# 52 spare matmuls of the identity with the mask in three places of TensorE's early queue, in a fused attention and feed-forward kernel

## The chip, the cores and the metric

The kernel runs on one core of one Trainium2 chip. The metric is the device time of one execution in microseconds, the median of three runs; lower is better. The engines are named as the profile names them: PE is TensorE, DVE is VectorE, ACT is ScalarE, POOL is GpSimd, SP is SyncE, which here only issues DMAs.

## The reference, cut to what matters

```python
# q, k, v: (B, H, S, D) = (4, 8, 576, 64); M_prev: (B, H, D, D); z_prev: (B, H, D)
scores = q @ k.T / sqrt(D), causal mask          # per batch and head
local  = softmax(scores) @ v
q_p    = where(q > 0, q, exp(q) - 1) + 1
mem    = (q_p @ M_prev) / (q_p . z_prev + 1e-6)
g      = sigmoid(beta)
x      = g * mem + (1 - g) * local               # (2304 tokens, 512)
h      = maximum(x @ w_in, 0)                    # w_in  (512, 2048)
out    = (h * h) @ w_out                         # w_out (2048, 512)
```

## The kernel before

**The tiling.** The 2304 tokens are cut into nine blocks of 256. Block 0 holds the first 64 tokens of each of the four batches; blocks 1 to 8 are two a batch. `first_tokens` computes the attention of block 0 (two groups `g`, each of two batches). `attention(b, p, tiles, ...)` computes the attention of the later tokens for batch `b` and head pair `p`. For batches 0 and 1 it runs twice a head pair, over the query tiles 1 and 2 (called lo below) and over the tiles 3 and 4 (hi). `moe(n)` is the feed-forward part of a block: "up" matmuls of 256 columns (L653 to L655, 192 a block) and "down" matmuls of 512 columns (L643 to L645, 96 a block). A product is made of three matmuls of high and low parts, so each weight is split once into two parts by ACT and DVE (`split_weight`, L163 to L169), and loaded in stages, as buffers come free.

**The order.** The program is recorded as a merge of `attention` for batch 0, lo, with the weight steps, then of `moe(0)` with more attention. A scheduler with a timeline of its own then sets the static order of each engine, and of the DMAs on SP's queue. Every engine works through its list in order, and what stands at its head waits for its operands. A change of the recorded program on one engine therefore changes the order on all of them.

**Buffers that the prediction speaks of.** Scores `sp` lie in a PSUM tile with the tag `s`, of which there is one, so the scores of the next group wait until DVE has read the last ones (L485). The tag `up` has two PSUM buffers, shared by the up products, the transposes `px` of the next block's tokens (L620, L622) and the transposes `px` and `pxa` of the first attention. Evacuation of `px` is done by ACT (`xh`, L625) and DVE (`xl`, L626). The tag `acc` has two PSUM buffers, those of the down products. The values `vv` of a head pair have one SBUF buffer, read by L399 and by L414 and L416.

**Operands of the new matmuls.** `identb` is the 128x128 identity in bf16, `mask` a 128x576 bf16 tile with 0 and -1e30; both exist before and are complete in the first 2.7 us.

Of the kernel before, what the change touches and what calls it, by code (L numbers as in the profile page):

```python
# [8 lines left out]
F32 = mybir.dt.float32  # L9
# [10 lines left out]
DM, FF = 512, 2048  # L20
NTOK = B * S
P = 128
# [50 lines left out]


FIRST = 4
AFTER = mybir.DependencyInfo(mybir.DependencyClass.NoSync, mybir.DependencyReason.DATA)
WHOLE = mybir.DependencyInfo(mybir.DependencyClass.Sync, mybir.DependencyReason.DATA)


def ORD(merge, attn, na, wsteps, first, order):  # L80
    merge((attn(0, 1), 12), (wsteps(13), 12))
    merge((attn(1, FIRST), 52), (wsteps(33), 20), (first(), 18))
    for _ in attn(FIRST, len(order)):
        pass
# [6 lines left out]
def fused_kernel(ctx: ExitStack, tc: tile.TileContext, t0_d, zt_d, kk_d, qv_d, beta, w_in, w_out, out):  # L91
    nc = tc.nc
# [5 lines left out]
    ps = ctx.enter_context(tc.tile_pool(name="ps", bufs=1, space=bass.MemoryType.PSUM))  # L98
# [6 lines left out]
    identb = cp.tile([P, P], BF16, name="identb")  # L105
    nc.vector.tensor_copy(identb, idt)
    mask = cp.tile([P, MW], BF16, name="mask")
# [87 lines left out]
    def weights():  # L195
        n0 = 0
        for n, ex in STG:
            n1 = n0 + n + len(ex)
            dpl = ctx.enter_context(tc.tile_pool(name=f"wd{n0}", bufs=1, reuse_waits="tile"))
            plain = range(n0 + len(ex), n1) if XF else range(n0, n0 + n)  # L200
            heads = []
            for m in range(n0, n1):
                if m in wt:
                    continue
                two = PAIR and m % 2 == 0 and m in plain and m + 1 in plain and m >= PAIR - 1
                wp[m] = dpl.tile([P, 2, 1024 if two else 512], F32R, name=f"w{m}")
                heads.append(m)
                for u in range(2 if two else 1):
                    wt[m + u] = wp[m][:, :, u * 512 : (u + 1) * 512]
            with ExitStack() as st:  # L210
                tp = st.enter_context(tc.tile_pool(name="tp", bufs=1, reuse_waits="tile")) if n0 == 0 else None
                spl = st.enter_context(tc.tile_pool(name=f"ws{n0}", bufs=1, reuse_waits="tile")) if n else None
                where = list(ex) + [spl] * n if XF else [spl] * n + list(ex)
                if n0 == 0:
                    first_tokens(tp, lambda: load_weight(heads[len(raw)], where[heads[len(raw)]]))
                    yield
                for m in range(n0, n1):
                    if m in heads:
                        if m not in raw:
                            load_weight(m, where[m - n0])  # L220
                        split_weight(m)
                    yield
            n0 = n1

    def first_tokens(tp, ahead):
        me, ze, se, xe, ye = ([nc.gpsimd if c == "p" else nc.vector for c in t] for t in TE)
        xh = mo.tile([P, NK, BLK], F32R, tag="xh", name="xh", bufs=2)
# [2 lines left out]
        ng = B // GB  # L230
        bc = [P, GN, D]
        tr, sp, wt0, wx = ({} for _ in range(4))
# [3 lines left out]
        for step in SEQ.split():  # L236
# [6 lines left out]
            else:  # L243
                g = int(step[1])
# [14 lines left out]
        def scores(g):  # L259
            sp[g] = sp0[:, g]  # L260
            qd = tr[g][:, : 2 * GD].rearrange("p (r i d) -> p i r d", r=2, i=GN)
            for i in range(GN):
                for h in range(2):
                    hd = slice(h * D, (h + 1) * D)
                    nc.tensor.matmul(sp[g][hd, i], qd[hd, i, 0], qd[hd, i, 1], start=True, stop=True)

        def phi(g):
            qn, zb = part(g, 2, 1), part(g, 3, 1)
            wt0[g] = tp.tile([P, GN, P], F32, tag="w", name="w", bufs=2)
            f = wt0[g][:, :, D:]  # L270
            t2 = tp.tile([P, GN], F32, tag="t2", name="t2", bufs=2)
            nc.scalar.activation(f, qn, AF.Exp)
            me[g].tensor_scalar(out=f, in0=f, scalar1=1.0, scalar2=None, op0=ALU.min)
            nc.vector.scalar_tensor_tensor(out=f, in0=qn, scalar=0.0, in1=f, op0=ALU.max, op1=ALU.add)
            ze[g].tensor_tensor(out=zb, in0=zb, in1=f, op=ALU.mult)
            nc.vector.reduce_sum(out=t2, in_=zb, axis=AX.X)
            nc.vector.tensor_scalar(out=t2, in0=t2, scalar1=1e-6, scalar2=None, op0=ALU.add)
            nc.vector.reciprocal(t2, t2)
            nc.vector.tensor_tensor(out=t2, in0=t2, in1=gpb, op=ALU.mult)
            se[g].tensor_tensor(out=f, in0=f, in1=t2[:, :, None].to_broadcast(bc), op=ALU.mult)  # L280
# [40 lines left out]

        sp0 = ps.tile([P, ng, GN, D], F32, tag="s", name="sp0")
        for g in range(ng):
            scores(g)
            phi(g)
        for g in range(ng):
            softmax(g)
# [18 lines left out]
    def attention(b, p, tiles, ld, after, early, sfull, full):  # L346
# [3 lines left out]
        tl = tiles[-1]  # L350
# [75 lines left out]
        for grp in (tiles[:2], tiles[2:]):  # L426
            ng = len(grp)
# [25 lines left out]
        row = {}  # L453

        def scores(group):
            sps = ps.tile([P, 2, 512], F32, tag="s", name="sp")
            c = 0
            at_col = []
            for i, ka, kb in group:
                qc = slice(QT[i][0] - D, sum(QT[i]) - D)  # L460
                cs = slice(c, c + kb - ka)
                at_col.append(cs)
                with tc.high_priority():
                    for x, (qt, kt) in enumerate(terms):
                        for h, hd in enumerate(heads):
                            mm = nc.tensor.matmul(  # L466
                                sps[:, h, cs], qt[hd, qc], kt[hd, ka:kb], start=x == 0, stop=x == len(terms) - 1
                            )
                            if behind:
                                tc.add_manual_dep(mm.ins, behind.pop().ins.name, AFTER, reason="a batch comes late")  # L470
                            while parts:
                                tc.add_manual_dep(mm.ins, parts.pop().ins.name, WHOLE, reason="a batch starts whole")
                c = cs.stop
            for (i, ka, kb), cs in zip(group, at_col):
                q0 = QT[i][0]
                if ka == 0:
                    row[i] = (
                        at.tile([P, 2, S], F32, tag="e", name="e", bufs=EB),
                        at.tile([P, 2, 2], F32, tag="mx", name="mx", bufs=4),
                        at.tile([P, 2], F32, tag="sm", name="sm", bufs=4),  # L480
                    )
                e, mx, _ = row[i]
                s = int(ka > 0)
                for h in range(2):
                    nc.vector.tensor_tensor_reduce(  # L485
                        out=e[:, h, ka:kb],
                        in0=sps[:, h, cs],
                        in1=mask[:, 448 - q0 + ka : 448 - q0 + kb],
                        scale=-0.125,
                        scalar=3e38 if s == 0 else mx[:, h, 0:1],  # L490
                        op0=ALU.add,
                        op1=ALU.min,
                        accum_out=mx[:, h, s : s + 1],
                    )

        for i in [t for t in TORD if t in tiles]:
            q0, n = QT[i]
            ke = q0 + n
            for group in SGROUP[i]:
                scores(group)  # L500
# [9 lines left out]
            if full:  # L510
# [3 lines left out]
                for b0 in range(0, 2 * nb, 4):  # L514
                    bn = min(4, 2 * nb - b0)
                    px = ps.tile([P, 4, P], F32, tag=PXT, name="pxa", bufs=2)
                    for x in range(bn):
                        h, c = divmod(b0 + x, nb)
# [38 lines left out]
            acc = ps.tile([P, 2, 2, D], F32, tag="av", name="acc", bufs=2)  # L557
            if full:
                s3 = acc[:, :, 0]
                for h in range(2):  # L560
                    hd = slice(h * D, (h + 1) * D)
# [143 lines left out]
                live[0][2] += 1  # L705

    blocks = [(None, 0)] + [(b, k) for b in range(B) for k in range(2)]
    xq, last, behind = [], [], []
    wg = weights()
    wn = [0]  # L710

# [21 lines left out]
    def attn(i0, i1):  # L733
        for i in range(i0, i1):
            ld = nxt.pop()

            def after():
                if i + 1 < len(order):
                    nxt.append(loads(*order[i + 1]))

            yield from attention(*order[i], ld, after, i < NEARLY, i < NES, i < NEF and max(order[i][2]) < 4)
# [67 lines left out]
```

## Time and profile before

| | us |
|---|---|
| median of three runs | 601.08 (600.86 to 603.04) |
| the profiled execution | 602.37 |
| its span, first to last instruction | 600.6 |
| PE busy in the span | 552.1 (92%) |
| DVE busy | 404.9 (67%) |
| ACT busy | 327.1 (54%) |

The profile is of one execution, whose own time lies 1.77 us above its span and 1.29 us above the median. Busy shares are averages over the whole span: DVE is full in the first part and nearly idle in the last quarter, PE the other way round, so the table alone doesn't say which engine sets the time. [...]

### The profile page before, as it was taken

Reading aid. Unit: us, or ns where it says so; the run is one execution under the profiler, and the core shown is the slowest. Engines: PE = TensorE matmul, PEld = TensorE weight load, DVE = VectorE, ACT = ScalarE, POOL = GpSimd, SP = SyncE. Lnnn points to the kernel's source line nnn. Section 1 sums busy time; section 2 is a strip of 40 time slices with the busy share of each in tenths; the row PEclk is TensorE's granted clock in tenths of the full one; section 3 lists DMA queues with packets and bytes.
Section 4 is the critical chain, followed back from the end, with each engine's and each line's share of the span. In section 5 each row is a group of like instructions: output and inputs, shape, how many; then the busy total and the mean of one; then the engine's idle time right before and its main releaser. Section 6 shows DMA issues by size and latency. Waiting matters only on the chain.

```text
span 600.6 us, 11532 instructions
## 1 busy us (share of the span) xinstructions
PE 552.1 (92%) x4198; PEld 482.5 (80%) x4198; DVE 404.9 (67%) x1285; ACT 327.1 (54%) x747; POOL 170.4 (28%) x139
## 2 busy tenths in 40 slices
PE   2478999799999999999999989999989999999997
PEld 2357887588888788788888888878879999998996
DVE  5999997888879798988789789897873001101000
ACT  3689885585767575855776646556351223213212
POOL 2502222044431424313332332223322321221221
PEclk9997999899999999999999999999999999999999
DMA  8947754666566575674565564564523100100000
GB/s 278 407 173 290 247 159 121 144 155 156 129 132 144 135 179 142 143 189 128 120 131 137 143 135 131 123 152 106 110 61 98 36 1 24 48 1 13 24 0 36
DMA packets 127576, 76.28 MB, mean 127 GB/s; under 512 B 99360, under 2 KB 112672, under 8 KB 127520
## 3 DMA queue, kind: packets, MB, share of 16 engines
q1 hardware_dynamic: 127520, 75.55, 47.6%
q8 instruction: 33, 0.54, 0.4%
q14 instruction: 23, 0.19, 0.1%
HBM read 42.63 MB, written 8.78 MB: 86 GB/s over the span
## 4 chain that ended last, share of the span: by engine, by line
PE 40%; DVE 31%; DMA 14%; ACT 8%; issue 4%; SPq 1%; POOL 1%; ACTq 0%; DVEq 0%
PE oacc L643 6%; PE oacc L645 6%; PE oacc L644 6%; PE up L653 6%; PE up L654 6%; PE up L655 6%; DVE a L545 5%; DVE e L485 4%; DMA vv<-in_qv_dram 4%; ACT e L505 3%; DMA aT<-a 3%; DMA qm<-in_qv_dram 3%; DVE w L169 3%; DVE memx L585 2%; PE sp L466 2%
## 5 line engine op out<-in xcount | busy, mean ns | idle before, releaser
L653 PE MATMUL up<-xh,w 128*128 128x256 f32 x576 | 167.2, 290 | 3.3 <-ACT aF L525 2.7
L654 PE MATMUL up<-xl,w 128*128 128x256 f32 x576 | 166.8, 290 | 0.0
L655 PE MATMUL up<-xh,w 128*128 128x256 f32 x576 | 165.8, 288 | 0.0
L668 POOL TENSOR_TENSOR gl<-r,gh 128x512 fp32r<-128x512 f32 x72 | 98.0, 1362 | 205.9 <-DVE gh L667 133.4
L505 ACT ACTIVATE e<-e,mx 128x320 f32<-128x320 f32 (+3 forms) x128 | 77.8, 609 | 86.3 <-DVE mx L485 45.0
L653 PEld LDWEIGHTS up<-xh,w 128*128 128x128 f32 x576 | 112.1, 195 | 8.3 <-ACT aF L525 3.1
L643 PE MATMUL oacc<-w,gh 128*128 128x512 f32 x288 | 115.5, 401 | 2.1 <-DVE gh L667 2.1
L654 PEld LDWEIGHTS up<-xl,w 128*128 128x128 f32 x576 | 112.2, 195 | 3.4 <-issue 0.9
L644 PE MATMUL oacc<-w,gh 128*128 128x512 f32 x288 | 113.8, 395 | 0.0
L655 PEld LDWEIGHTS up<-xh,w 128*128 128x128 f32 x576 | 112.2, 195 | 1.4 <-issue 0.4
L645 PE MATMUL oacc<-w,gl 128*128 128x512 f32 x288 | 110.5, 397 | 0.3 <-POOL gl L668 0.3
L661 POOL TENSOR_TENSOR r<-r 128x512 f32<-128x512 f32 x40 | 48.0, 1199 | 160.1 <-ACT r L659 156.4
L659 ACT ACTIVATE r<-up 128x512 f32<-128x512 f32 x72 | 42.2, 587 | 93.6 <-PE up L655 86.0
L667 DVE CAST gh<-r 128x512 fp32r<-128x512 f32 x40 | 16.9, 422 | 109.0 <-ACT r L663 108.0
L545 DVE SCALAR_TENSOR_TENSOR a<-e,a 128x128 f16<-128x128 f32 x120 | 71.8, 620 | 26.4 <-ACT a L543 26.1
L643 PEld LDWEIGHTS oacc<-w,gh 128*128 128x128 f32 x288 | 54.4, 189 | 12.3 <-DVE gh L667 2.4
L645 PEld LDWEIGHTS oacc<-w,gl 128*128 128x128 f32 x288 | 53.3, 188 | 13.3 <-issue 1.7
L644 PEld LDWEIGHTS oacc<-w,gh 128*128 128x128 f32 x288 | 54.4, 189 | 8.5
L543 ACT ACTIVATE a<-e 128x128 f16<-128x128 f32 x120 | 55.7, 519 | 4.3 <-DMA aT<-a 3.3
L485 DVE CUSTOM_DVE_ANT_0 e<-sp,mask 128x320 f32<-128x320 f32 (+3 forms) x128 | 47.5, 413 | 0.1
L575 PE MATMUL acc<-vs,aT 128*128 128x128 f16 x308 | 36.9, 220 | 0.0
L572 PE MATMUL acc<-vs,aT 128*128 128x64 f16 x308 | 35.5, 193 | 0.0
(127 smaller groups left out, 873.6 us busy)
## 6 DMA issues: line engine op xcount, KB each, us to landing
raw<-in_w_in_dram SPq DMA_DIRECT2D x11, 512.0 KB, 7.4
vv<-in_qv_dram SPq DMA_DIRECT2D x16, 320.0 KB, 3.3
raw<-in_w_out_dram SPq DMA_DIRECT2D x9, 512.0 KB, 7.0
kd<-in_kk_dram SPq DMA_DIRECT2D x16, 288.0 KB, 3.2
out_dram<-o SPq DMA_DIRECT2D x16, 256.0 KB, 2.0
xd<-memx SPq DMA_DIRECT2D x31, 128.0 KB, 1.9
xn<-xd SPq DMA_DIRECT2D x14, 256.0 KB, 2.8
qm<-in_qv_dram SPq DMA_DIRECT2D x8, 321.0 KB, 3.1
```

The costliest lines, as they stand in the source:

```text
L485: nc.vector.tensor_tensor_reduce(out=e[:, h, ka:kb], in0=sps[:, h, cs], in1=mask[:, 448 - q0 + ka : 448 - q0 + kb], scale=-0.125, scalar=3 ...
L505: ex = nc.scalar.activation(e[:n, h, :ke], e[:n, h, :ke], AF.Exp, bias=bs, scale=-1.0, accum_out=sm[:n, h : h + 1])
L543: nc.scalar.mul(av[:, :, o0 : o0 + w], x, SC)
L545: nc.vector.scalar_tensor_tensor(out=av[:, :, o0 + w : o0 + 2 * w], in0=x, scalar=SC, in1=av[:, :, o0 : o0 + w], op0=ALU.mult, op1=ALU.sub ...
L643: nc.tensor.matmul(acc[t], gh[:, u, ts], w_out_op(f, 0), start=f == 0, stop=False)
L644: nc.tensor.matmul(acc[t], gh[:, u, ts], w_out_op(f, 1), start=False, stop=False)
L645: nc.tensor.matmul(acc[t], gl[:, u, ts], w_out_op(f, 0), start=False, stop=f == NF - 1)
L653: nc.tensor.matmul(up[:, u, :], w_in_op(f, k, 0), xh[:, k, :], start=k == 0, stop=False)
L654: nc.tensor.matmul(up[:, u, :], w_in_op(f, k, 0), xl[:, k, :], start=False, stop=False)
L655: nc.tensor.matmul(up[:, u, :], w_in_op(f, k, 1), xh[:, k, :], start=False, stop=k == NK - 1)
L661: nc.gpsimd.tensor_tensor(out=r, in0=r, in1=r, op=ALU.mult)
L668: nc.gpsimd.tensor_tensor(out=gl, in0=r, in1=gh.bitcast(F32), op=ALU.subtract)
```

## The change

`spin(n, ins)` issues `n` matmuls of `identb` with the first 512 columns of `mask` into a PSUM tile `spun` with the tag `acc`, which nothing reads. Each has a dependency on an instruction that only orders the two in the schedule, and makes no engine wait. It is called three times: 14 after the scores of the second group of the first tokens, 28 after the scores of batch 0, pair 0, lo, and 10 ahead of the scores of batch 0, pair 2, lo, after DVE's read of the scores before them.

```diff
+SPIN = [14, 28, 10]
...
+    def spin(n, ins):
+        if not spun:
+            spun.append(ps.tile([P, DM], F32, tag="acc", name="spun", bufs=2))
+        for _ in range(n):
+            mm = nc.tensor.matmul(spun[0], identb, mask[:, :DM], start=True, stop=True)
+            tc.add_manual_dep(mm.ins, ins.ins.name, AFTER, reason="keeps the clock")
+
+    spun = []
+
     def first_tokens(tp, ahead):
...
         for g in range(ng):
-            scores(g)
+            mm = scores(g)
+            if g == ng - 1:
+                spin(SPIN[0], mm)
             phi(g)
...
         def scores(group):
+            if (b, p) == (0, 2) and tl == 2:
+                with tc.high_priority():
+                    spin(SPIN[2], reads[0])
             sps = ps.tile([P, 2, 512], F32, tag="s", name="sp")
...
+            if (b, p) == (0, 0) and tl == 2:
+                spin(SPIN[1], mm)
...
-                    nc.vector.tensor_tensor_reduce(
+                    read = nc.vector.tensor_tensor_reduce(
...
+                    if c == cs.stop and h == 0:
+                        reads[:] = [read]
```

Three places show how the static order changes. Lines of the change are numbered 10 to 20 higher than those of before: L466 is then L482, L485 is L503, L653 is L673.

The first place is PE's queue at the start. Before, the scores of the first tokens (L265) and of pair 0 (L466) are followed by the transposes of the first tokens' weights (L304):

```order
L265 MATMUL sp_155<-tr_118 64x64 x16
L265 MATMUL sp_155<-tr_119 64x64 x16
L466 MATMUL sp<-kd,qm 128x320 x2
L466 MATMUL sp<-kd,qm 128x192 x2
L304 MATMUL px_221<-identr,w 128x128 x4
```

With the change 14 pairs of a weight load and a matmul (L230) stand ahead of pair 0's scores, and 28 behind them; one pair of each stands here:

```order
L275 MATMUL sp_155<-tr_118 64x64 x16
L275 MATMUL sp_155<-tr_119 64x64 x16
L230 LDWEIGHTS identb
L230 MATMUL spun<-mask,identb 128x512
...
L482 MATMUL sp<-kd,qm 128x320 x2
L482 MATMUL sp<-kd,qm 128x192 x2
L230 LDWEIGHTS identb
L230 MATMUL spun<-mask,identb 128x512
...
L315 MATMUL px_236<-identr,w 128x128 x4
```

The third ten stand between the last transposes of pair 1 (L540) and the first up matmul of block 0; nothing else is new on PE.

The second place is PE's queue at the end of block 0, at batch 0, pair 1, hi. Before, its second scores (512 columns) follow its first ones (448 and 64 columns) with only `vt`, `pm` and two transposes between them:

```order
L466 MATMUL sp<-kd,qm 128x448 x2
L466 MATMUL sp<-kd,qm 128x64 x2
L403 LDWEIGHTS vx
L403 MATMUL vt<-identb,vx 128x128
L434 MATMUL pm<-qm,pe 128x130 x2
L622 MATMUL px<-identr,memx 128x128 x2
L466 MATMUL sp<-kd,qm 128x512 x2
L653 MATMUL up<-xh,w_1003 128x256
```

With the change the transposes of the next block have moved here too, and 38 up matmuls stand ahead of the second scores:

```order
L482 MATMUL sp<-kd,qm 128x448 x2
L482 MATMUL sp<-kd,qm 128x64 x2
L640 MATMUL px<-identr,xn 128x128 x3
L642 MATMUL px<-identr,memx 128x128
...
L416 LDWEIGHTS vx
L416 MATMUL vt<-identb,vx 128x128
L447 MATMUL pm<-qm,pe 128x130 x2
L673 MATMUL up<-xh,w_1056 128x256
...
L674 MATMUL up<-xl,w_98 128x256
L482 MATMUL sp<-kd,qm 128x512 x2
```

Both orders have 252 feed-forward matmuls ahead of the 448-column scores. Ahead of the next pair's first scores (pair 2, hi) there are 296 before and 322 with the change. Ahead of the memory product `pm` of batch 1, pair 1, lo, there are 549 and 535, and ahead of the last attention's `pm` 1648 and 1653.

The third place is DVE's queue at the same time. Before, the reduction of the values of pair 0, hi (L399) stands ahead of the reads of that pair's 512-column scores (L485):

```order
L545 SCALAR_TENSOR_TENSOR a<-e,a 128x2x64
L545 SCALAR_TENSOR_TENSOR a<-e,a 128x2x384
L399 TENSOR_REDUCE vx<-vv 128x1
L485 ISA e,mx<-sp,mask,mx 128x512
L485 ISA mx 128x1
L485 ISA e,mx<-sp,mask,mx 128x512
L485 ISA mx 128x1
L401 TENSOR_SCALAR vx<-vx 128x1
L389 SCALAR_TENSOR_TENSOR pe<-qm,pe 128x256
```

With the change those reads (L503), the last weight parts (L170) and the sums of `acc` (L597) stand ahead of it (L412):

```order
L503 ISA e,mx<-sp,mask,mx 128x512
L503 ISA mx 128x1
L503 ISA e,mx<-sp,mask,mx 128x512
L503 ISA mx 128x1
L170 TENSOR_TENSOR w_1207<-xw,w_1207 128x256
L402 SCALAR_TENSOR_TENSOR pe<-qm,pe 128x256
L170 TENSOR_TENSOR w_1207<-xw,w_1207 128x256
L597 TENSOR_REDUCE s_980<-acc 128x128
L597 TENSOR_REDUCE s_1012<-acc 128x128
L412 TENSOR_REDUCE vx<-vv 128x1
L565 SCALAR_TENSOR_TENSOR a<-e,a 128x2x64
L605 SCALAR_TENSOR_TENSOR memx<-s_980,sm,memx 128x64 x2
```

The last weight part is row 224 of DVE's list before and row 245 with the change; weights come later, attention of batch 0 earlier.

## Rows read from the trace of the kernel before

**Rows 1.** The page, 40 slices of 15.0 us: granted TensorE clock, tenths.

```profile
PEclk9997999899999999999999999999999999999999
```

**Rows 2.** Busy time by stretch: us, then engines, granted clock, DMA share, GB/s.

```profile
40.00:60.00 20.00, 15.33 (x81) 13.76 (x81) 20.00 (x56) 18.44 (x44) 3.12 (x2) 0.75 0.82 309
...
60.00:80.00 20.00, 20.00 (x133) 17.84 (x133) 20.00 (x50) 17.63 (x46) 4.51 (x3) 0.99 0.76 216
...
150.00:200.00 50.00, 47.52 (x396) 42.12 (x395) 41.81 (x153) 33.17 (x91) 17.05 (x15) 1.00 0.61 140
```

**Rows 3.** The same view in short stretches, where the clock fell and rose.

```profile
43.00:44.00 1.00, 1.00 (x8) 0.78 (x4) 1.00 (x4) 0.87 (x4) 0.00 (x0) 0.58 1.03 373
49.00:50.00 1.00, 1.00 (x6) 1.00 (x6) 1.00 (x3) 1.00 (x6) 0.00 (x0) 0.50 1.02 416
56.00:57.00 1.00, 0.66 (x5) 0.66 (x6) 1.00 (x5) 1.00 (x4) 0.54 (x1) 0.91 0.14 53
60.00:61.00 1.00, 1.00 (x9) 1.00 (x9) 1.00 (x4) 0.81 (x4) 0.00 (x0) 0.88 0.00 0
...
114.00:116.00 2.00, 2.00 (x12) 1.50 (x9) 1.97 (x10) 1.98 (x5) 0.00 (x0) 0.71 0.96 191
118.00:120.00 2.00, 2.00 (x28) 1.96 (x27) 1.39 (x4) 0.90 (x2) 0.00 (x0) 0.93 0.42 156
```

**Rows 4.** PE's timeline, 8 to 57 us: start, us, instruction, count, [idle before, releaser].

```profile
8.90 1.98 PE L265 MATMUL sp<-tr 64*64 64x64 f32 x32 [2.59 <-DMA tr<-in_t_dram]
16.12 2.08 PE L466 MATMUL sp<-kd,qm 64*128 64x320 f32 x8 [5.25 <-DVE raw L163]
24.46 1.97 PE L304 MATMUL px<-identr,w 128*128 128x128 f32 x8 [6.27 <-POOL w L295]
...
37.66 0.87 PE L520 MATMUL pxa<-identr,e 128*128 128x128 f32 x6
...
42.11 1.14 PE L466 MATMUL sp<-kd,qm 64*128 64x320 f32 x8 [2.04 <-DVE mx L485]
...
56.34 0.39 PE L653 MATMUL up<-xh,w 128*128 128x256 f32 x1 [1.52 <-ACT aF L525]
```

**Rows 5.** PE's timeline, two down matmuls of 512 columns at the full clock.

```profile
65.44 0.39 PE L644 MATMUL oacc<-w,gh 128*128 128x512 f32 x1
65.67 0.39 PE L645 MATMUL oacc<-w,gl 128*128 128x512 f32 x1
```

**Rows 6.** ACT's timeline at the transposes of the first tokens.

```profile
26.16 0.60 ACT L306 COPY wx<-px 128x512 f32<-128x512 f32 x1
```

**Rows 7.** PE's timeline, 108 to 123 us.

```profile
108.04 1.19 PE L466 MATMUL sp<-kd,qm 64*128 64x448 f32 x8 [0.94 <-DVE mx L485]
...
113.45 1.13 PE L466 MATMUL sp<-kd,qm 64*128 64x512 f32 x4 [3.24 <-DVE mx L485]
...
116.98 0.41 PE L653 MATMUL up<-xh,w 128*128 128x256 f32 x1
117.19 0.41 PE L654 MATMUL up<-xl,w 128*128 128x256 f32 x1
...
118.39 0.28 PE L654 MATMUL up<-xl,w 128*128 128x256 f32 x1
118.51 0.28 PE L655 MATMUL up<-xh,w 128*128 128x256 f32 x1
...
122.94 0.47 PE L466 MATMUL sp<-kh,qh 64*128 64x448 f32 x2
```

**Rows 8.** DVE's timeline, 105 to 114 us.

```profile
105.82 0.82 DVE L399 TENSOR_REDUCE vx<-vv 128x1 f32<-128x640 f32 x1 [2.51 <-DMA vv<-in_qv_dram]
106.56 0.74 DVE L485 CUSTOM_DVE_ANT_0 e<-sp,mask,mx 128x512 f32<-128x512 f32 x1
...
111.66 0.62 DVE L485 CUSTOM_DVE_ANT_0 e<-sp,mask 128x448 f32<-128x448 f32 x1
...
113.38 0.68 DVE L626 TENSOR_TENSOR xl<-px,xh 128x512 fp32r<-128x512 f32 x1
```

More of the change, by code (lines that the diff above doesn't have):

```diff
@@ L264, in scores @@
                     hd = slice(h * D, (h + 1) * D)
-                    nc.tensor.matmul(sp[g][hd, i], qd[hd, i, 0], qd[hd, i, 1], start=True, stop=True)
+                    mm = nc.tensor.matmul(sp[g][hd, i], qd[hd, i, 0], qd[hd, i, 1], start=True, stop=True)
+            return mm
         def phi(g):
@@ L707, in fused_kernel @@
     blocks = [(None, 0)] + [(b, k) for b in range(B) for k in range(2)]
-    xq, last, behind = [], [], []
+    xq, last, behind, reads = [], [], [], []
     wg = weights()
```

## The prediction

> **What bounds the kernel now.** I read the page's slices first, for the clock; then busy times by stretch, for the engine that is full in each; then PE's timeline where the clock falls; then DVE's timeline at the one long wait behind it. The line of the granted clock [rows 1] shows it under full in slices 4 (45 to 60 us) and 8 (105 to 120 us). In short stretches [rows 3] the edges follow from the mixture of 1.0 and 0.5: at 0.58 in 43 to 44 us the clock fell at 43.16; it is 0.50 until 50; 0.91 in 56 to 57 and 0.88 in 60 to 61 put the second stretch at 56.82 to 60.24; 0.71 and 0.93 put the third at 114.84 to 118.28. [...] Each fall comes behind gaps: 2.04 us before the scores at 42.11 and 1.52 before 56.34 [rows 4], 0.94 and 3.24 before 108.04 and 113.45 [rows 7].
>
> The start is a fourth such stretch, which the granted clock doesn't show, since its records say 1.00 there. The same eight score matmuls took 2.08 us at 16.12 and 1.14 us at 42.11 [rows 4], so PE was at half speed at 16 us and at full speed at 42.
>
> What that half speed costs is another matter. From 40 to 80 us DVE is busy for 20.00 of 20.00 us twice, and ACT for 18.44 in the first of them [rows 2]: they split weights and evacuate scores, and PE waits for them. From 60 to 80 us PE is busy 20.00 of 20.00 too. So up to about 80 us the engines are close to each other, DVE first. Then a wait decides: at 103.3 us DVE stops for 2.51 us for the load of `vv`, with the reads of the 512-column scores queued behind it [rows 8]; these free the PSUM buffer for the scores at 108.04, and the next scores wait 3.24 us for DVE again [rows 7]. From there PE is nearly full (47.52 of 50 us in 150 to 200 us, [rows 2]), so what PE has in hand at about 123 us, together with how little attention makes it wait later, is the end time.
>
> **The change part by part.** *The spare matmuls.* No row has a bf16 matmul of 512 columns. The nearest are the down matmuls of 512 columns, 0.23 us from start to start at full clock [rows 5]; from full to half clock 256 columns go from 0.12 to 0.21 us [rows 7], so 512 should take about 0.43. I take 0.23 and 0.43; the end below is the 0.12 of 256 columns, above it 0.46, twice the down matmul. The 14 take 6.0 us at half and 3.2 at full speed, in a gap from 10.88 (8.90 + 1.98) to 16.12 us, 5.2 us long. The 28 take 12.0 or 6.4 us, in a gap from 18.20 to 24.46 us, 6.3 us long. The 10 take 4.3 or 2.3 us, in a gap from 38.53 (37.66 + 0.87) to 42.11 us [rows 4]. Two of the three slow stretches of [rows 3] lasted 3.4 us with PE busy all through; if the first call is the like, its clock is up at about 14.3 us, and the gaps hold the calls: cost nothing, covered by PE's waits for DMA, DVE and POOL. Without that cover they cost what they overrun.
>
> *The clock up to 50 us.* Then PE is at full speed from about 14 us on, and the fall at 43.16 is gone: there PE has 3.4 us less to do by 50 us. Between 16 and 38 us its work shortens too, but the weight splits fill DVE without a break, so that is worth 0 by itself. The second stretch, 56.82 to 60.24, stands behind waits for ACT, which no call fills; I take 0 for it, with 1.7 as the upper bound.
>
> *The order at 105 us.* This is where a gain can become lasting. In the new order the reads of the 512-column scores stand ahead of the reduction that waits for `vv`. The load can't come earlier, since its buffer is freed at the same point of DVE's list; the reads can. They move into the 2.51 us of waiting. Two reads cost about 1.4 us (106.56 to 107.90 in [rows 8], the second like the first). Small steps move with them (`pe` and the sums of `acc`); my estimate is that they fill 2.3 of the 2.51 us, so that what follows on DVE comes 2.3 us earlier, and the 448-column scores at 111.66 are read near 109.4 instead.
>
> On PE, 38 up matmuls now stand ahead of the second scores. They need PSUM from `up`, which the transposes hold until DVE's L626 (113.38, [rows 8]); that instruction moves ahead of the reads. So PE starts them near 109.4 us too. At 0.12 us each they take 4.6 us and the scores start at 114.0, or at 115.4 if the clock falls once more in the gap before (11 at 0.12, 16 at 0.21, 11 at 0.12, 6.0 us); before, they started at 113.45 [rows 7]. Counted at the first scores of pair 2, hi, which ran at 122.94 [rows 7], the new order has 322 feed-forward matmuls done instead of 296. The 26 more are 14 of 0.12 and 12 of 0.23 us: 1.7 + 2.8 = 4.5 us of PE work in hand, with those scores at about the same time (the delay of 0.6 to 2.0 us in the second scores is balanced by no slow stretch, or one shorter than 3.44 us, behind them).
>
> *How much of it lasts.* By the memory product of batch 1, pair 1 the new order has 14 feed-forward matmuls fewer ahead of it than before, and by the last attention 5 more. So attention has to catch up by the 4.5 us, or PE waits for it. DVE is busy for 41.81 of 50 us in 150 to 200 us [rows 2], so 8 us of slack in that stretch alone, but PE already lost 2.5 us there to waits. I take 80% as lasting: 0.8 x 4.5 = 3.6 us. The ends are 0 and 4.5 plus what remains of the 3.4 us, about 8.
>
> **The sum.** 602.37 - 3.6 = 598.8 us for the profiled execution (600.6 in the span and 1.77 around it). That execution lies 1.29 above the median of the runs shown, so the forecast for the median is 601.08 - 3.6 = 597.5 us.
>
> [...] The rows show a slow stretch at the start whose end is seen only in durations, somewhere between 16.12 and 42.11 us [rows 4]. [...]
>
> **The rivals.** *First, nothing comes of it.* DVE and ACT are full to 80 us [rows 2], so PE's faster clock only makes it wait longer, and the 4.5 us in hand at 123 us are given back by 200 us, since attention, held by DVE and its loads, comes no sooner. For it: the orders agree again (549 against 535, 1648 against 1653). Against it: the 3.24 us wait [rows 7] lies behind DVE's wait for `vv` [rows 8], which the new order uses. Time: 601.1, within 1.5.
>
> *Second, the new order waits more later.* Every engine's list is new to the end, and PE's waits in 150 to 450 us depend on it. Another 1 us in each of the six stretches like that of [rows 2] would be 6, less the 3.6 gained: 603.5.
>
> *Third, slower by overrun.* If the clock is still at half speed through the 28, they take 12.0 us from 18.20 (or later) and end at 30.2 instead of 24.46; the transposes of the first tokens come 5.7 us late. ACT has the copy of these in its list at 26.16 [rows 6] and would wait, with the weights' casts behind it, and DVE behind those. ACT's copy is some 2 us later in the new list, so 3.5 us reach DVE, which has no slack up to 80 us [rows 2]. Time: 601.1 + 3.5 = 604.6 at most, if nothing is gained behind it. It decides from an end of the 28 later than about 28 us.
>
> **How the numbers follow.** The forecast has 0.66, of which 0.50 ends under 598.1 (faster by over 0.5%, 3.0 us, about what a measurement of this kernel can tell from no change) and 0.16 between 598.1 and 600. The first rival has 0.18, all within 0.5%. The second has 0.06, half of it slower. The third has 0.10, of which 0.09 is slower. So faster 0.50, same 0.38, slower 0.12. The likeliest case alone has 593 to 600. The range that leaves out 2 in 10 reaches from 593.0 (8 us gained) to 603.0, which takes in the first rival and half of the second.
>
> **What would show it.** Right: the granted clock at 1.0 from 43 to 50 us; the eight scores near 16 us in 1.1 to 1.2 us; 52 matmuls of L230, the 28 ending before 25 us; DVE full as before up to 80 us; the 512-column scores of pair 1, hi, at 114 to 115.4 us with 290 feed-forward matmuls done; the first scores of pair 2, hi, near 123 us or earlier, with 322. Wrong: the 28 still running at 28 us; ACT idle at its first copy of `wx`; a vv wait on DVE as long as the 2.51 us of before; PE's waits in 150 to 450 us longer by more than 3 us. What would make it wrong in size: attention that reaches pair 2, hi, earlier than 123 us, which would make the gain larger, or a new long gap on PE with a new fall of the clock.

## The result, and the profile after

The changed kernel takes 606.89 us (606.36 to 608.07, six runs), the kernel before beside it 602.23 us: a ratio of 1.0084, 95% interval 1.0061 to 1.0108. It is slower by 0.84%, where 0.6% faster was forecast. The profiled execution took 608.07 us, its span is 606.3.

The page of the changed kernel, PE's busy time and the granted clock (tenths of full speed) in 40 slices of 15.2 us:

```profile
PE 561.0 (93%) x4248; PEld 482.3 (80%) x4250; DVE 405.8 (67%) x1285; ACT 328.5 (54%) x747; POOL 177.2 (29%) x139
...
PEclk9889998899999999999999999999999999999999
```

The slow slices 4 and 8 of [rows 1] are now 2, 3, 7 and 8. By stretch (us, then PE, PEld, DVE, ACT, POOL busy, granted clock, DMA share, GB/s):

```profile
20.00:25.00 5.00, 2.99 (x14) 1.17 (x12) 5.00 (x23) 3.07 (x10) 0.90 (x1) 1.00 1.03 410
25.00:30.00 5.00, 1.97 (x8) 1.57 (x8) 5.00 (x11) 2.11 (x5) 3.17 (x3) 0.51 0.94 370
30.00:35.00 5.00, 4.07 (x40) 3.30 (x40) 4.97 (x12) 4.36 (x9) 0.00 (x0) 0.50 0.03 13
35.00:40.00 5.00, 4.95 (x58) 3.75 (x59) 5.00 (x14) 5.00 (x14) 0.00 (x0) 0.97 0.15 36
40.00:60.00 20.00, 18.72 (x130) 15.83 (x128) 19.62 (x57) 19.43 (x50) 3.52 (x3) 1.00 0.90 334
60.00:80.00 20.00, 19.11 (x121) 16.22 (x120) 16.78 (x52) 16.22 (x43) 7.44 (x4) 1.00 0.60 176
100.00:120.00 20.00, 17.20 (x110) 14.15 (x111) 15.92 (x55) 11.95 (x27) 3.88 (x3) 0.83 0.56 132
```

From 40 to 60 us the clock is full (1.00), where it fell twice before [rows 3]. But it is at half from about 25 to 35 us (0.51 and 0.50), and 0.83 in 100 to 120 us, read as a mixture of 1.0 and 0.5, is half for 6.8 of the 20 us, against 3.44 before. PE's timeline shows the waits at the fall at 25:

```profile
15.70 1.14 PE L482 MATMUL sp<-kd,qm 64*128 64x320 f32 x8 [2.03 <-DMA qm<-in_qv_dram]
16.77 6.22 PE L230 MATMUL spun<-mask,identb 128*128 128x512 bf16 x28
25.72 1.97 PE L315 MATMUL px<-identr,w 128*128 128x128 f32 x8 [2.73 <-POOL w L306]
30.93 1.12 PE L326 MATMUL xp<-wx,tr 128*64 128x64 f32 x16 [3.25 <-ACT wx L317]
...
116.87 1.13 PE L482 MATMUL sp<-kd,qm 64*128 64x512 f32 x4
...
124.92 0.47 PE L482 MATMUL sp<-kh,qh 64*128 64x448 f32 x2
```

The eight scores take 1.14 us instead of 2.08 [rows 4], and the 28 spares end at 22.99, both as forecast. Behind them PE waits 2.73 and 3.25 us for POOL and ACT, whose work the new order has put later: the first copy of `wx` starts at 30.31 us, at 26.16 before [rows 6]. The half clock behind these waits is no loss against the kernel before, which was at half there too, though its granted clock says 1.00 from 20 to 40 us: its transposes at 24.46 us took the same 1.97 us [rows 4], and its next eight scores 2.08 us, where the changed kernel's took 1.13 at 36.36. The kernel before:

```profile
25.00:30.00 5.00, 3.83 (x31) 2.91 (x31) 5.00 (x13) 4.53 (x9) 2.59 (x2) 1.00 1.01 398
30.00:35.00 5.00, 4.59 (x42) 3.47 (x42) 5.00 (x12) 3.96 (x9) 0.00 (x0) 1.00 0.06 20
```

```profile
34.39 2.08 PE L466 MATMUL sp<-kd,qm 64*128 64x320 f32 x8
```

Pair 1 hi's scores start at 116.87 (forecast 114.0 to 115.4, before 113.45 [rows 7]), and pair 2 hi's at 124.92 with 322 feed-forward matmuls done, against 122.94 with 296. The 26 more are worth 4.5 us by the prediction's prices; 2.0 us later, they leave 2.5 us in hand, not 4.5. The reduction of `vv`, which waited 2.51 us before [rows 8], waits for nothing now. But the transposes ahead of the up matmuls wait for the load of `xn` (issued at 106.08 us, at 100.14 before), and DVE then for ACT. So the up matmuls start at 110.84 us, not at 109.4 as forecast, and take 6.0 us with one more fall of the clock (0.50 from 111 to 113 us). DVE's and PE's rows, in order of time:

```profile
104.58 0.82 DVE L412 TENSOR_REDUCE vx<-vv 128x1 f32<-128x640 f32 x1
108.85 0.45 PE L640 MATMUL px<-identr,xn 128*128 128x128 f32 x3 [2.06 <-DMA xn<-xd]
110.10 0.69 DVE L646 TENSOR_TENSOR xl<-px,xh 128x512 fp32r<-128x512 f32 x1 [2.52 <-ACT xh L645]
110.84 0.58 PE L673 MATMUL up<-xh,w 128*128 128x256 f32 x1 [0.36 <-DVE xl L646]
```

SP's queue has moved too. The loads of the third part of the weights (`raw`, `hw`, `xw`), issued from 61.85 to 69.0 us before, now stand behind `kd`, `vv` and two transposes:

```profile
63.74 0.34 SPq L349 DMA_DIRECT2D kd<-in_kk_dram  x1
67.28 0.33 SPq L356 DMA_DIRECT2D vv<-in_qv_dram  x1
67.71 3.17 SPq L569 DMA_TRANSPOSE aT<-a  x2
71.56 0.47 SPq L194 DMA_DIRECT2D raw<-in_w_out_dram  x1
```

DVE, full from 60 to 80 us before [rows 2], is busy for 16.78 of 20 us. And yet the head is not where the time went, as the experiments show: it is the stretch behind 120 us. PE's waits from 120 to 480 us (total, times, longest), the changed kernel:

```profile
PE acc L590 <- DVE memx L456: 5.9, 6, 2.0
PE sp L482 <- DVE ql L377: 4.3, 6, 1.1
PE sp L482 <- DVE vx L414: 2.1, 2, 1.4
PE oacc L665 <- POOL gl L688: 2.0, 4, 0.7
```

and a second profile of the kernel before, taken by the control below:

```profile
PE sp L482 <- DVE ql L377: 2.9, 5, 1.0
PE acc L590 <- DVE memx L456: 2.9, 3, 1.2
PE oacc L663 <- DVE gh L687: 2.1, 2, 1.5
PE acc L590 <- DVE vs L429: 1.6, 2, 1.1
```

From 150 to 450 us PE idles for 13.3 us in the first profile of the kernel before and for 17.9 in the changed kernel, some 4.5 us more. The prediction named 3 us more as a sign of being wrong.

```profile
150.00:450.00 300.00, 286.69 (x2361) 249.42 (x2359) 255.31 (x864) 186.28 (x447) 94.12 (x74) 1.00 0.57 133
```

```profile
150.00:450.00 300.00, 282.14 (x2315) 243.85 (x2315) 251.89 (x833) 178.62 (x430) 92.78 (x71) 1.00 0.58 133
```

### The profile page after: what moved, and what is told of

It reads as the page before. It is cut to its first block, busy times and chain, and to the rows that moved or that the text cites. A ratio compares the mean times of both kernels' runs of the same rounds, so it can differ in the third digit from the quotient of the medians.

```text
span 606.3 us, 11643 instructions
## 1 busy us (share of the span) xinstructions
PE 561.0 (93%) x4248; PEld 482.3 (80%) x4250; DVE 405.8 (67%) x1285; ACT 328.5 (54%) x747; POOL 177.2 (29%) x139
## 4 chain that ended last, share of the span: by engine, by line
DVE 36%; PE 34%; DMA 14%; ACT 9%; issue 5%; SPq 1%; POOL 0%; ACTq 0%; DVEq 0%
DVE a L565 7%; DVE e L503 5%; PE up L675 5%; PE up L674 5%; PE up L673 5%; PE oacc L664 5%; PE oacc L665 5%; PE oacc L663 5%; DMA vv<-in_qv_dram 4%; ACT e L525 4%; DMA aT<-a 4%; DVE memx L605 3%; ACT a L563 3%; DMA qm<-in_qv_dram 2%; DVE vs L429 2%
## 5 line engine op out<-in xcount | busy, mean ns | idle before, releaser
L673 PE MATMUL up<-xh,w 128*128 128x256 f32 x576 | 165.5, 287 | 1.4 <-DVE xl L646 1.2
L674 PE MATMUL up<-xl,w 128*128 128x256 f32 x576 | 165.0, 286 | 0.0
L688 POOL TENSOR_TENSOR gl<-r,gh 128x512 fp32r<-128x512 f32 x72 | 104.0, 1445 | 193.0 <-DVE gh L687 124.7
L673 PEld LDWEIGHTS up<-xh,w 128*128 128x128 f32 x576 | 110.5, 192 | 4.6 <-DVE xl L646 1.5
L674 PEld LDWEIGHTS up<-xl,w 128*128 128x128 f32 x576 | 110.6, 192 | 3.5 <-issue 1.1
L675 PEld LDWEIGHTS up<-xh,w 128*128 128x128 f32 x576 | 110.5, 192 | 2.3 <-issue 1.5
L565 DVE SCALAR_TENSOR_TENSOR a<-e,a 128x128 f16<-128x128 f32 x120 | 75.1, 644 | 30.8 <-ACT a L563 30.4
L503 DVE CUSTOM_DVE_ANT_0 e<-sp,mask 128x320 f32<-128x320 f32 (+3 forms) x128 | 47.4, 414 | 0.6 <-PE sp L482 0.6
L605 DVE SCALAR_TENSOR_TENSOR memx<-s,sm,memx 128x64 f32<-128x64 f32 x120 | 36.8, 356 | 0.2
```

The costliest lines, as they stand in the source:

```text
L503: read = nc.vector.tensor_tensor_reduce(out=e[:, h, ka:kb], in0=sps[:, h, cs], in1=mask[:, 448 - q0 + ka : 448 - q0 + kb], scale=-0.125, s ...
L565: nc.vector.scalar_tensor_tensor(out=av[:, :, o0 + w : o0 + 2 * w], in0=x, scalar=SC, in1=av[:, :, o0 : o0 + w], op0=ALU.mult, op1=ALU.sub ...
L605: nc.vector.scalar_tensor_tensor(out=xo, in0=s3[:n, h], scalar=sm[:n, h : h + 1], in1=xo, op0=ALU.mult, op1=ALU.add,)
L673: nc.tensor.matmul(up[:, u, :], w_in_op(f, k, 0), xh[:, k, :], start=k == 0, stop=False)
L674: nc.tensor.matmul(up[:, u, :], w_in_op(f, k, 0), xl[:, k, :], start=False, stop=False)
L675: nc.tensor.matmul(up[:, u, :], w_in_op(f, k, 1), xh[:, k, :], start=False, stop=k == NK - 1)
```

## The experiments

Each ratio is to the kernel before on the same chip, with its 95% interval. The five sets ran on four chips; the kernel before took 601.5, 601.8, 603.4, 601.0 and 600.9 us there. "Old" and "new order" are the orders of the kernel before and of the changed kernel.

### Order and spare matmuls taken apart

The theory after the result: the new order behind 120 us loses the time, not the spares. The rival: the spares do, by the clock or by what they delay. To part them, the order on all five queues is fixed by ordering dependencies on the schedule, read from a table:

```diff
     with _tile.TileContext(nc, schedule_with_timeline_sim=True) as tc:
         fused_kernel(tc, *args)
+        fixed_order(tc)
...
+            if last is not None:
+                tc.add_manual_dep(ins[p], ins[last].name, AFTER, reason="fixed order")
```

The table holds one of the two orders, or one for all that each engine had started by 120 us (the head) and the other behind (the tail), each with and without the 52 spares. A kernel with one head and the other tail has a seam that no scheduler planned; what the seam costs is not told apart from the tail or the head.

The control, the old order written out:

> A control: the kernel before with its own order written out, which is the same program. It shows how far two sets of runs of one program lie apart, and a second profile of it, how far two executions of one program drift apart on the way. Expected: a ratio of 1.000 within 0.003; if the drift along the way is some us, what single traces show of gains and losses after 200 us is not a property of the kernels.

Ratio 0.9993 (0.9971 to 1.0016). The first four:

> The changed kernel's order of instructions on every engine's queue, written out by hand, with the 52 spare matmuls left out of it; nothing else differs. Theory (the new order loses the time, the spare matmuls do not): slower than before by as much as the changed kernel or more, 606 to 610 us, and TensorE is half clocked in the gaps again, near 43 and 57 us. Rival (the spare matmuls and the slow clock behind them, 25 to 35 us, cost it): back at the time of before or a little above, 601 to 603 us.

> The order of the kernel before on every engine's queue, with the 52 spare matmuls put in at the same three places of TensorE's queue (their neighbours there are the same in both orders). Theory (the order loses the time): no slower than before; if the clock that the spare matmuls hold is worth what the prediction says, 598 to 600 us, if it is worth nothing, 601 to 602.5 us. Rival (the spare matmuls cost it): 605 to 608 us, as the changed kernel.

> With the spare matmuls; each queue has the changed kernel's order for all that the changed kernel had started by 120 us, and behind it the rest in the order of the kernel before. Theory that the order after 120 us loses the time (TensorE idle there 13.7 us before, 19.0 us in the changed kernel): 599 to 602 us, with about 14 us idle behind 120 us. Rival that the head loses it (weights of the feed-forward asked for 7 to 10 us later, which the tail then pays): 605 to 607 us.

> With the spare matmuls; each queue has the order of the kernel before for all that it had started by 120 us, and behind it the rest in the order of the changed kernel. Theory that the order after 120 us loses the time: 604 to 607 us, with about 19 us of idle TensorE behind 120 us. Rival that the head loses it: 599 to 602 us.

And the two that complete the square:

> The same queues as the kernel that had the changed kernel's order up to 120 us and the old order behind it, without the spare matmuls. So far, against before: old order with spares +0.67%, new head and old tail with spares +0.21%, old head and new tail with spares +1.44%, new order without spares +0.64%. Theory (three effects that add up: the new tail costs about 4 us, the spares about 1 to 4 us, the new head gives about 3 us back): 598.5 to 601.5 us. Rival (the new head is only good with the spares, for which it was planned): 602.5 to 605 us.

> The old order up to 120 us and the changed kernel's order behind it, without the spare matmuls: the tail's cost by itself. Theory (the new order behind 120 us costs about 4 us whatever is ahead of it): 604.5 to 607 us. Rival (the tail costs only behind the spares or the new head): 601 to 602.5 us.

| head, tail | no spares | 52 spares |
|---|---|---|
| old, old | 1 (the kernel before) | 1.0067 (1.0037 to 1.0097) |
| new, old | 0.9979 (0.9960 to 0.9998) | 1.0021 (0.9992 to 1.0049) |
| old, new | 1.0119 (1.0077 to 1.0161) | 1.0144 (1.0108 to 1.0180) |
| new, new | 1.0064 (1.0038 to 1.0089) | 1.0084 (1.0061 to 1.0108), the change |

The new tail costs 1.19, 0.85, 0.77 and 0.63% in the four pairs that differ in it alone, 0.86% on the mean: 5.2 us. The new head gives 0.21, 0.55, 0.46 and 0.60%, mean 0.46%: 2.7 us. The 52 spares cost 0.67, 0.42, 0.25 and 0.20%, mean 0.39%: 2.3 us. The sum, 0.79%, is close to the change's 0.84%. Of the pairs, those within one set and chip are the firmest: for the tail 1.19 and 0.77%, for the head 0.21 and 0.46%, for the spares 0.67%. So the theory holds for the tail, the largest of the three terms; it fell where it held the spares harmless, and the rival has part of the loss. The spares' cost here takes in that of the PSUM tile they write, which the kernels without spares lack; a single spare with that tile gains 0.31% (below).

Part of the tail's loss shows in the stretch from 280 to 430 us: the second profile of the old order, then the new order, then the old head with the new tail, all without spares; the first and the third ran on one chip.

```profile
280.00:430.00 150.00, 143.88 (x1186) 125.90 (x1184) 127.53 (x424) 88.94 (x215) 45.39 (x36) 1.00 0.57 130
```

```profile
280.00:430.00 150.00, 142.03 (x1166) 123.26 (x1167) 124.66 (x416) 87.08 (x207) 45.83 (x36) 0.99 0.54 126
```

```profile
280.00:430.00 150.00, 141.50 (x1163) 122.81 (x1162) 124.35 (x414) 88.33 (x211) 46.24 (x35) 0.99 0.55 127
```

PE idles for 6.1 us in the first and for 8.0 and 8.5 in the others (9.4 in the changed kernel), and the clock of 0.99 there is one more fall, between 280 and 350 us (0.98 there in both, 1.00 behind it) (PE's longest wait for `memx` between 120 and 480 us is 1.8 and 2.0 us in them, and 1.2 in the first). That is 2 to 3 of the 5.2 us, and not in every pair: with the spares in front, the old order idles for 8.8 us there too, and its clock is lower:

```profile
280.00:430.00 150.00, 141.19 (x1135) 123.08 (x1134) 119.76 (x398) 85.02 (x202) 41.73 (x34) 0.97 0.56 122
```

From 120 to 480 us PE idles longer with the new tail in all four pairs, by 2.0, 0.8, 2.7 and 4.3 us. The rest of the 5.2 us is not traced to a wait.

### One spare fewer

```diff
-SPIN = [14, 28, 10]
+SPIN = [13, 28, 10]
```

> The changed kernel with 13 spare matmuls in the first gap in place of 14, the order left to the scheduler, which plans every queue anew. Theory (most of the result is which order the scheduler happens to come to): more than 1.5 us from the changed kernel's 606.9 us, to either side, anywhere from 598 to 610 us. Rival (the spare matmuls themselves cost it): 606 to 608 us.

1.0155 (1.0127 to 1.0182), 610.88 us. One spare of 0.23 us fewer moves the time by 0.7%, almost as much as the change did: the scheduler comes to another order for every queue.

### What the spares themselves do

All in the old order, so that no queue's order moves.

> The order of the kernel before on every queue with the first two groups of spare matmuls alone (14 and 28), the ten left out. Against the 605.4 us with all 52 in that order and 601.5 us with none. Theory (nothing is to be had before 100 us, and what is lost is lost to falls that other waits bring): 602 to 605 us. Rival (the ten alone did the harm, the first two cost nothing): 601 to 602 us.

1.0042 (1.0024 to 1.0061).

> The order of the kernel before on every queue, none of the 52 spare matmuls, and instead 40 short ones (128 columns, into an unused third of a memory-read tile) on TensorE's queue between the transposes at 109.9 us and pair 1 hi's 512-column scores at 114.0 us, the one gap of the kernel before whose fall of the clock (114.84 to 118.28 us) stands where VectorE waits for TensorE. Theory (a fall costs only where TensorE is waited for): 599 to 600.5 us, 1 to 2.3 us less than before. Rival (spare work only moves the falls to later waits): 601 to 604 us.

```diff
+            spares[k] = [
+                nc.tensor.matmul(pm[:, 2, :P], identb, mask[:, :P], start=True, stop=True).ins
+                for _ in range(SPARE.get(k, (0, 0))[0] if ng < 3 else 0)
+            ]
```

0.9999 (0.9980 to 1.0018). In its profile the fall at 114.84 is gone (up matmuls start 0.12 us apart from 113.19 us on, 0.21 apart in that fall [rows 7]), and the second scores start at 111.91 us (at 113.45 and 111.51 in the two profiles of the kernel before):

```profile
108.50 2.40 PE L451 MATMUL pm<-mask,identb 128*128 128x128 bf16 x40
111.91 1.13 PE L488 MATMUL sp<-kd,qm 64*128 64x512 f32 x4 [1.01 <-DVE mx L509]
```

Behind them PE is idle for 2.6 us from 120 to 280 us, against 5.8 before, and then for 10.6 from 280 to 430 us:

```profile
120.00:280.00 160.00, 157.44 (x1284) 136.94 (x1285) 137.30 (x481) 109.20 (x261) 59.27 (x45) 1.00 0.68 155
...
280.00:430.00 150.00, 139.42 (x1149) 120.94 (x1149) 122.89 (x406) 85.05 (x203) 41.73 (x34) 1.00 0.52 123
```

What PE had in hand was waited away at a clock of 1.00. So the forecast of this run fell: the removal of the fall gained nothing. It is no test of the theory, since the first profile of the kernel before shows no engine waiting for TensorE at that fall; DVE is busy for 3.41 of its 3.44 us:

```profile
114.84:118.28 3.44, 3.44 (x19) 3.44 (x18) 3.41 (x14) 1.14 (x3) 0.00 (x0) 0.50 0.93 233
```

(How much of the 10.6 us is the chip's is left open below.) The next try, at the other two gaps:

> The order of the kernel before on every queue, none of the 52 spare matmuls, and instead 26 short ones right ahead of the scores at 42.11 us and 18 right ahead of the feed-forward's first matmuls at 56.34 us: the falls at 43.16 and 56.82 us should be gone, which the prediction priced at 3.4 us and nothing. Theory (VectorE, busy 5.00 us of every 5 between 20 and 60 us, sets the pace there): 601 to 602.5 us although both falls are gone. Rival (the prediction's price): 597.5 to 599 us. If spare work only moves falls to later: 603 to 605 us.

1.0087 (1.0055 to 1.0118), but the run answers another question. The spares wrote an unused third of `pm`, the reader of `pm` waited for the tile's last writer, and DVE lost 2.61 us at 40 us:

```profile
40.62 0.16 DVE L456 SCALAR_TENSOR_TENSOR nm<-pm,gi 128x4 f32<-128x4 f32 x1 [2.61 <-PE pm L451]
```

So it was run again with the spares in a tile of their own, then repeated and taken apart:

> The spares at 40 and 55 us once more, in the old order, now into the tile that the change gives them: in the run before, VectorE's read of the memory tile waited 2.61 us for the spares that shared it, so that run did not tell what the falls at 43 and 57 us are worth. Here 8 full-width spares ahead of the scores at 42.11 us and 6 ahead of the matmuls at 56.34 us. The prediction's price: both falls gone, 597.5 to 599 us. Theory (VectorE sets the pace there): 601 to 602.5 us.

> The kernel with 8 spares at 40 and 6 at 55 us in the old order once more, on another chip, beside its parts. It was 0.86% faster than before (598.7 against 603.4 us), though its profile still has TensorE at half clock for 10.3 us (49.8 to 60.1 us). If that gain is real: a ratio of 0.989 to 0.995 again. If it was the chip: 0.997 to 1.003.

> The old order with a single spare matmul, ahead of the scores at 42.11 us: it holds no clock, but like all of the change's kernels it takes one turn of the two down-projection tiles in PSUM, so each later one lies in the other of the two. Theory A (the gain of the last run is that turn, since at the same clock the kernels with it in the old tail were some 2 to 3 us faster): a ratio of 0.990 to 0.996. Theory B (the gain is the clock held at 43 and 57 us): 0.998 to 1.002.

> The 8 spares ahead of the scores at 42.11 us alone, old order. By the prediction's price of the fall at 43.16 us (3.4 us) and theory B: a ratio of 0.993 to 0.997. Theory A: as the single spare, 0.990 to 0.996 too. VectorE sets the pace: 0.998 to 1.002.

> The 6 spares ahead of the feed-forward's matmuls at 56.34 us alone, old order. The prediction priced the fall at 56.82 us at nothing: by that and theory B 0.997 to 1.002, all of the gain being the first fall's. Theory A: as the single spare, 0.990 to 0.996.

| spares, old order | ratio |
|---|---|
| 8 at 40 us and 6 at 55 us | 0.9914 (0.9882 to 0.9945), again 0.9919 (0.9893 to 0.9945) |
| 8 at 40 us | 0.9923 (0.9895 to 0.9951), 596.96 us |
| 6 at 55 us | 0.9965 (0.9943 to 0.9986) |
| one at 40 us | 0.9969 (0.9950 to 0.9989) |
| 14 behind the first products | 0.9947 (0.9930 to 0.9963) |
| 28 behind the scores of pair 0 | 0.9938 (0.9917 to 0.9960) |

The single spare holds no clock (0.58 in 40 to 50 us, row below) and gives 0.31%, between what theory A and theory B forecast. The six at 55 give no more than it. That does not price the fall at 57 us, since in the profile of the single spare the clock is at 1.00 there already (0.95 in 50 to 60 us with the six); the single spare's row:

```profile
55.00:60.00 5.00, 4.08 (x32) 3.82 (x32) 5.00 (x15) 5.00 (x14) 2.81 (x2) 1.00 0.19 60
```

The eight at 40 us give 0.46% or 2.8 us more than the single one (2.4 us by the medians), though the intervals touch. In the old order, kernels with some of the spares beat both kernels.

The eight do not remove the fall, they move it. PE, clock and the rest, first with one spare, then with eight:

```profile
40.00:50.00 10.00, 8.41 (x36) 7.67 (x37) 10.00 (x30) 9.03 (x24) 0.00 (x0) 0.58 1.00 394
50.00:60.00 10.00, 8.49 (x58) 7.43 (x57) 10.00 (x26) 9.55 (x23) 3.52 (x2) 0.91 0.51 179
```

```profile
40.00:50.00 10.00, 7.34 (x49) 5.54 (x49) 9.71 (x30) 7.82 (x20) 0.00 (x0) 1.00 0.91 354
50.00:60.00 10.00, 7.38 (x34) 6.29 (x35) 10.00 (x27) 10.00 (x24) 2.49 (x2) 0.56 0.69 268
```

Nor does DVE come sooner by it. The same two rows of DVE's list in the second profile of the old order, with a single spare, and with the eight:

```profile
76.16 0.55 DVE L412 TENSOR_REDUCE vx<-vv 128x1 f32<-128x384 f32 x1
...
103.89 0.82 DVE L412 TENSOR_REDUCE vx<-vv 128x1 f32<-128x640 f32 x1 [2.47 <-DMA vv<-in_qv_dram]
```

```profile
76.95 0.54 DVE L412 TENSOR_REDUCE vx<-vv 128x1 f32<-128x384 f32 x1
...
104.25 0.82 DVE L412 TENSOR_REDUCE vx<-vv 128x1 f32<-128x640 f32 x1 [2.39 <-DMA vv<-in_qv_dram]
```

```profile
76.94 0.55 DVE L412 TENSOR_REDUCE vx<-vv 128x1 f32<-128x384 f32 x1
...
104.33 0.82 DVE L412 TENSOR_REDUCE vx<-vv 128x1 f32<-128x640 f32 x1 [2.10 <-DMA vv<-in_qv_dram]
```

The eight are no earlier than the single spare. The two profiles of the old order without spares lie further apart, at 103.89 here and at 105.82 in [rows 8]. So where the eight gain their 2.8 us is not shown.

The last two runs tried to find which group of the change does harm:

> The old order with the first group of the change alone, 14 spares behind the first products (in the gap of 10.88 to 16.12 us). With 14 and 28 together the ratio was 1.0042, with a single spare 0.9969: the two groups cost about 0.7% beside the turn of the tile. If the 14 do it: 1.002 to 1.006. If they do nothing: 0.995 to 0.999, as the single spare. If they gain by the earlier full clock: below 0.995.

> The old order with the second group alone, 28 spares behind pair 0's scores (in the gap of 18.20 to 24.46 us). If the 28 do the harm: 1.002 to 1.006. If they do nothing: 0.995 to 0.999. If a warm TensorE in 24 to 36 us gains: below 0.995.

0.9947 (0.9930 to 0.9963) and 0.9938 (0.9917 to 0.9960). Neither does harm: each alone gains, though the intervals overlap with the single spare's. Together (1.0042) they do not, and all 52 (1.0067) less still. This is not settled. The runs with 14 and 28 and with all 52 were on other chips than the runs of single groups, and were not repeated there; and all five profiles of the old tail from these first two sets, that of the run at 110 us included, have PE idle for 8.8 to 10.6 us in 280 to 430 us, against 4.6 to 6.3 in those of the later sets and 5.9 in the first profile of the kernel before. That may be the chip, though the new tail's profiles on one of these chips (8.0 and 8.5 us) don't differ so from that on another (8.5); the kernel before was timed on those chips (601.5 and 601.8 us) but not profiled there. In the profile of all 52 in the old order the clock falls in places where the kernel before has none: it is 0.91 in 300 to 320, in 320 to 340 and in 400 to 420 us. Over the twelve runs of that kernel the time goes with the clock: 601.9 to 603.1 us for four of the five fastest clocks (0.979 to 0.988), 608.7 and 609.1 for the two slowest (0.972 and 0.971).

## Why the prediction was wrong

**The slow stretches and the cost of a spare: right.** 0.23 us each, 6.22 for 28, no overrun; the third rival did not come.

**"PE is at full speed from about 14 us on": wrong.** Behind the first 14 PE was at full speed (the eight scores took 1.14 us, 2.08 before), but the order then made it wait 2.73 and 3.25 us behind the 28, and it was at half clock from 25 to 35 us (0.51 and 0.50). The prediction looked at the gaps that the spares fill and not at the new ones. The half clock there is not what made the kernel slower: the kernel before had it too.

**"The fall at 43.16 is gone", 3.4 us: gone, and its price not shown for the change.** The 3.4 us are half of the 6.84 us from 43.16 to 50 us, by the clock of 0.50 [rows 3], as the bound of 1.7 for the fall at 56.82 is half of its 3.42. Eight spares at that gap alone gave 2.8 us over a single one, but with the fall moved to 50 to 60 us (0.56 there) and not gone. The 0 for the fall at 57 us was not tested. And in the old order the change's ten, further from the scores, which ended at 38.9 us with the scores at 41.68, did not hold the clock there (0.50 in 45 to 50 us, half from 41.7 to 51.9 us by the mixture), and all 52 cost 0.67%.

**The order at 105 us, 4.5 us in hand: the mechanism right, the size off.** DVE's wait for `vv` is gone and 322 feed-forward matmuls are done ahead of pair 2, hi. In hand were 2.5 us in the profile, and the new head, all that stands ahead of 120 us, is worth 2.7 us by the four pairs. What ate the rest: the second scores came 3.42 us later instead of up to 2; the 1.4 us between are the later start of the up matmuls, behind the load of `xn` and ACT. Nor was DVE full up to 80 us, as the prediction expected (it was busy for 16.78 us of the last 20), and the weight loads went behind the transposes on SP's queue, a move that the sum did not count; what that cost is not shown.

**"80% lasts": the step that failed.** It spoke of attention catching up in the order as it was. The order behind 120 us was new as well, and by itself costs 5.2 us, more than the head gives. That is the second rival, which had a chance of 0.06 and 603.5 us: its loss of 6 us was about right (5.2 by the experiments, some 4.5 as PE's waits from 150 to 450 us), but its chance stood against the prediction's own sentence that every engine's list is new to the end. And the 3.6 us it set against that were 2.7, less 2.3 for the spares.

The falls that the prediction took from one profile differ in another execution of the kernel before. Of the two slow stretches between 40 and 65 us in its second profile the first lasts 10.2 us, up to 51 us, and the second 3.4 us, where the first profile has 6.84 and 3.42 us [rows 3]. The second profile there:

```profile
40.00:45.00 5.00, 3.48 (x15) 2.85 (x15) 5.00 (x18) 3.97 (x12) 0.00 (x0) 0.58 0.96 338
45.00:50.00 5.00, 5.00 (x23) 4.88 (x24) 4.98 (x14) 4.20 (x11) 0.00 (x0) 0.50 1.02 393
50.00:55.00 5.00, 4.23 (x26) 3.34 (x25) 5.00 (x13) 4.79 (x11) 0.07 (x1) 0.90 1.03 404
55.00:60.00 5.00, 3.48 (x22) 3.44 (x22) 5.00 (x15) 5.00 (x13) 2.54 (x2) 0.79 0.26 89
60.00:65.00 5.00, 5.00 (x28) 4.21 (x28) 5.00 (x16) 4.03 (x14) 0.05 (x1) 0.87 0.47 128
```

## What to carry to other kernels

Where a scheduler sets the order, an edit at the front is two changes: the edit, and a new order for everything behind it. Fix the old order and put the edit into it before judging the edit; here one spare matmul fewer moved the time by 0.7%, and parts of the edit in the fixed order gained 0.5 to 0.6%, where all of it cost 0.67%. And a fall of the clock that is gone from a trace is not yet time gained: taking away the one at 114.84 us gave 0.9999. So measure what a filled gap is worth with the order held.

## What the runs showed of the hardware

- One program's falls of the clock differ between executions in place and length: 6.84 us at half clock between 40 and 55 us in one profile of the kernel before, 10.2 in the other.
- With a single spare matmul in the old order, into a PSUM tile of its own, the kernel ran in 0.9969 (0.9950 to 0.9989) of the time. In the program that tile is recorded ahead of all PSUM tiles but the first scores', so later tiles may lie elsewhere. No trace shows where they lie, and whether that is the cause was not tried.
- The granted clock of a trace can say 1.00 where TensorE is at half: in the kernel before it is 1.00 in every stretch of 5 us up to 40 us, and yet eight score matmuls take 2.08 us at 16.12 and 34.39 us and 1.14 at 42.11.
- A fall of the clock (0.50 from 114.84 to 118.28 us), in which VectorE was busy for 3.41 of 3.44 us, was removed by spares without any gain in the end (0.9999, 0.9980 to 1.0018).
